# Pairs of tiles from tile 6, row tiles turned later in a step, pair sums used a product later, transfers spread over steps

## The chip, the cores and the metric

The kernel runs on one core of one Trainium2 chip. A core has five engines that run their own instruction streams side by side: TensorE (PE, matrix products), VectorE (DVE), ScalarE (ACT), GpSimd (POOL) and SyncE (SP, which here only issues transfers). Each runs its instructions in the order in which they were written and waits at an instruction until what it needs is there. The metric is the device time of one execution in microseconds (us). Three executions before the change took 1418.22, 1418.4 and 1423.74 us; their median is 1418.4.

## What is computed

A sequence of 2048 rows of 512 features goes through two layers, each a linear-attention block (A) and a gated block (B), with a layernorm ahead of each and a residual around it:

```python
def _B_ref(x, w_in, w_sp, b_sp, w_out):
    z = _gelu(jnp.einsum("bsd,df->bsf", x, w_in))
    z1 = z[..., :Fh]
    z2 = _layernorm(z[..., Fh:], axis=-1)
    g = jnp.einsum("ts,bsf->btf", w_sp, z2) + b_sp[None, :, None]
    return jnp.einsum("bsf,fd->bsd", z1 * g, w_out)

x = A_x
x = x + _A_ref(_layernorm(x, axis=-1), A_wqkv, A_wo)
x = x + _B_ref(_layernorm(x, axis=-1), B_w_in, B_w_sp, B_b_sp, B_w_out)
x = x + _A_ref(_layernorm(x, axis=-1), A_wqkv, A_wo)
x = x + _B_ref(_layernorm(x, axis=-1), B_w_in, B_w_sp, B_b_sp, B_w_out)
```

Fh is 896. The stage that the change is in computes the end of A (query side, output weights, residual), the layernorm, and both halves of `z`: `z1` and the raw `z2`.

## The kernel before

Every matrix product is done in three passes: both operands are split into a high part (ACT rounds it, L101) and a low part (DVE subtracts, L104), and PE multiplies high by high, high by low and low by high (`mm3`, L115 to L117). The 2048 rows are 16 tiles of 128. Each layer runs `P1` (keys, values), `transition`, `P2`, and `P4` (the spatial product and the output). All order is written out by hand: an engine runs its instructions in program order.

`P2.run` goes through steps s = 1 to 18, a software pipeline in which one step works on several tiles:

- `b_high(s)`, `b_low(s)`: the scaled queries of tile s, which went to DRAM and back to be turned by blocks, are transposed on DVE (L351) and split.
- `a2_den`, `a2_mul` (tile s+2), `a` (tile s+3, on POOL, L657): the queries' denominators and scaling. `a2_mul` stores the turned queries to DRAM through SP.
- `c(s-1)`: 12 matmuls with the folded output weights; `c2`: DVE adds the residual (L713); `c_stats`: layernorm statistics on DVE (L287, L289), then three tiny POOL instructions (L291, L292, L294); `c3`: x is stored (L721), ACT normalises (L300), and the row tile is stored turned to DRAM (L336). `xturn.load(s-1)` loads it back through SP, which can only start when the store has landed.
- `d_high(s-2)`, `d_low(s-2)`: DVE transposes that row tile, ACT and DVE split it. Every four tiles make up one block n of `xT`.
- `e`, `e2`, `e3`, `e4` (`singly`): the second half of `z` for one tile (24 matmuls of 448 columns on two banks), its GELU (L927), its layernorm statistics, and the normalisation (with a subtraction on DVE, L938, for tiles 0 to 7).
- `f`: one "z1 unit": 12 matmuls of 512 columns for one of seven feature groups of one block of four tiles, a GELU on ACT (L959), a store (L962). A block's seven units are queued when its fourth tile has been split; up to two are taken per step. So in steps 9, 13 and 17 only one is left in the queue. In layer two the split weights of a unit are loaded from DRAM by POOL (L185, `Parts`), two units ahead: taking one starts the load of the one after the next.

In layer two, from step 7 on, two tiles are done together with seven products where eight would be needed (a Strassen-Winograd scheme on 2x2 blocks). `odd(s)` begins pair m with P1 and P2, `even(s)` goes on with P6, P5, P7, P4 and P3. Each is six matmuls of 448 columns (L804 to L806). P1, P6, P7 and P4 accumulate one after the other in one PSUM bank X, and ACT copies X out after P1 (L849), P6 (L877), P7 (L891) and P4 (L899); DVE adds the other banks (`add`, L816). P6, P5, P7 and P3 need sums of the pair's two row tiles: `block_sums` (four DVE instructions, L762 to L765) and `block_parts` (their splits; P6 and P5 use the first two parts). They need the row split of the pair's second tile, which `d_high` and `d_low` make in the same odd step. The weight sums T1 to T4 are loaded by POOL (L262, `Sums2.fetch`), two per step in steps 2 to 5.

After step 18 `P4.run` first takes the five z1 units that are left, prepares the first operands of the spatial product and finishes the last pair (`finish`), then PE starts the spatial product, whose first step needs all eight PSUM banks.

Of the kernel before, what the change touches and what calls it, by code (L numbers as in the profile page):

```python
# [19 lines left out]
NT = S // P  # L20
# [4 lines left out]
LN_EPS = 1e-5  # L25
PHI_EPS = 1e-6
DEFER = 6


class Slots:  # L30
# [23 lines left out]
def mixer_kernel(ctx: ExitStack, tc: tile.TileContext, x_in, wqkv, wo_d, win1_d, win2_d, wsp_d, bsp_d, wout_d,  # L54
# [17 lines left out]
    def ztag(i, shape, kind, dtype=F32):  # L72
        t = main.tile(shape, dtype, tag=f"z{i}", bufs=1, name=f"z{i}_{kind}")
        ztile[i] = t
        return t
# [27 lines left out]
    def low(l, src, h):  # L103
        nc.vector.tensor_sub(l, src, h.bitcast(F32))  # L104
# [16 lines left out]
    def flush(n=4):  # L121

        for _ in range(min(n, len(stores))):
            d, part, page = stores.popleft()
            nc.sync.dma_start(d, part.bitcast(F32))
            if page is not None:
                pages.put(page)
# [145 lines left out]
    def w_wo():  # L273
        return Weight(bigs, [P, 4, 512], [wo_d[c * P:(c + 1) * P, :] for c in range(4)])
# [4 lines left out]
    def w_in2():  # L279
        return Weight(bigs, [P, 4, FH], [win2_d[f] for f in range(NF)])  # L280
# [75 lines left out]
    class P1:  # L356
        def __init__(self, L):
# [4 lines left out]
            self.wo, self.win2 = w_wo(), w_in2()  # L362
            self.later = deque(range(NT - DEFER, NT))
            self.turn = Turn(f"xt{L}", range(3) if L == 0 else ())
# [156 lines left out]
        def run(self):  # L521
            side = deque()
            for w in (self.wv, self.wo, self.win2):
                side.extend([w] * len(w.pieces))
            side[0].fetch()
            ND = NT - DEFER
            for s in range(1, NT + 2):
                self.loadx(s + 3)
                self.turn.load(s + 1)
                flush()  # L530
                turned = 2 <= s < NT and s not in self.turn.by_pe
                if turned:
                    self.T_high(s)
                if s == 1:
                    if not self.kb:
                        self.K(0)
                    self.K(1)
                elif 2 < s <= NT:
                    self.K(s - 1)
                self.ln_a(s + 2)  # L540
                if turned:
                    self.T_low(s)
                if s <= NT:
                    self.K_phi(s - 1)
                if s <= ND:
                    self.Q(s - 1)
                if s == NT + 1:
                    self.late()
                if s <= NT:
                    self.xsplit(s - 1)  # L550
                    self.K_split(s - 1)
                if s + 1 < NT and s + 1 in self.turn.by_pe:
                    self.T(s + 1)
                self.ln_b(s + 2)
                if s <= ND:
                    self.Q_phi(s - 1)
                if s >= 2:
                    self.Gmm(s - 2)
                if s == NT + 1:
                    self.late_phi()  # L560
                for _ in range(min(len(side), 1 if s < 6 else 2)):
                    side.popleft().piece()
                for w in list(side)[:1 if s < 5 else 2]:
                    w.fetch()
# [71 lines left out]
    class P2:  # L636
# [105 lines left out]
        def d_low(self, i):  # L742
            b, home, h, l = self.dpart
            low(l, b, h)
            if self.sums2 is not None and i >= 4:
                self.rows.append(b)
            else:
                home.put(b)
            n, k = divmod(i, 4)
            if i in self.xB:  # L750
                pages.put(self.xB.pop(i))
            if k == 3:
                self.fnext = [(n, f) for f in range(NF)]
# [63 lines left out]

        def last_quarter(self, m):

            if m < 2:  # L820
                return
            self.add(2 * m, self.HI, self.Z)
            banks.put(self.Z)
            self.gelu(2 * m, self.HI)

        def two(self, step, m):
            if m >= 2:
                step(2 * m)
                step(2 * m + 1)

        def odd(self, s):
            m = (s - 3) // 2
            i = 2 * m
            if s < NT:
                self.b_high(s)
                self.b_low(s)
            self.a2_den(s + 2)
            self.d_high(s - 2)
            self.d_low(s - 2)
            self.two(self.e4, m - 2)  # L840
            self.last_quarter(m - 1)
            if s <= NT:
                self.c(s - 1)
                self.c2(s - 1)
                self.c_stats(s - 1)
            self.X, y = banks.get([P, HF]), banks.get([P, HF])
            self.product(self.X, m, "P1", start=True)
            z = ztag(i, [P, FH], f"z{self.L}")
            nc.scalar.activation(z[:, self.LO], self.X, AF.Copy)  # L849
            self.product(y, m, "P2", start=True, stop=True)  # L850
            self.a2_mul(s + 2)
            if s <= NT:
                self.c3(s - 1)
            self.a(s + 3)
            self.block_sums(m)
            self.add(i, self.LO, y)
            banks.put(y)
            self.block_parts(m)
            self.gelu(i, self.LO)
            self.xturn.load(s - 1)  # L860
            self.f()
            self.f()

        def even(self, s):
            m = (s - 4) // 2
            i, X = 2 * m, self.X
            if s < NT:
                self.b_high(s)
                self.b_low(s)
            self.a2_den(s + 2)  # L870
            if s <= NT:
                self.c(s - 1)
                self.c2(s - 1)
                self.c_stats(s - 1)
            Z = self.Z = banks.get([P, HF])
            self.product(X, m, "P6")
            nc.scalar.activation(ztile[i][:, self.HI], X, AF.Copy)  # L877
            self.product(Z, m, "P5", start=True)
            self.a2_mul(s + 2)
            if s <= NT:  # L880
                self.c3(s - 1)
            self.a(s + 3)
            if s <= NT + 1:
                self.d_high(s - 2)
                self.d_low(s - 2)
            self.f()
            if m >= 3:
                self.e3(i - 2)
            self.product(X, m, "P7")
            z = ztag(i + 1, [P, FH], f"z{self.L}")  # L890
            nc.scalar.activation(z[:, self.HI], X, AF.Copy)  # L891
            self.add(i + 1, self.HI, Z)
            self.gelu(i + 1, self.HI)
            if m >= 3:
                self.e3(i - 1)
            self.xturn.load(s - 1)
            self.f()
            self.product(X, m, "P4", stop=True)
            nc.scalar.activation(z[:, self.LO], X, AF.Gelu_apprx_tanh)  # L899
            banks.put(X)  # L900
            self.product(Z, m, "P3", stop=True)
            pages.put(*self.S_pages)
# [63 lines left out]
        def run(self, sums):  # L966
            for s in range(1, NT + 3):
                self.loadx(s + 1)
                self.qturn.load(s + 1)
                flush()  # L970
                paired = self.sums2 is not None and s >= 7
                if paired:
                    if s == 7:
                        self.e4(3)
                    (self.odd if s % 2 else self.even)(s)
                else:
                    self.singly(s)
                self.fq.extend(self.fnext)
                self.fnext = []
                if self.L == 0:  # L980
                    self.win1.piece(True)
                    self.win1.fetch()
                    if s > 7:
                        sums.tick()
                else:
                    if 2 <= s < 6:
                        self.sums2.fetch(2)
                    if s == 4:
                        self.win1.fetch()
                if s >= NT + 1:  # L990
                    self.p4.fetch(s - NT - 1)
            if self.L == 0:
                self.e4(NT - 1)
            else:
                self.sums2.free()
            self.win2.free()
# [372 lines left out]
    sums = Sums()  # L1369
# [44 lines left out]
```

## Time and profile before

| | |
|---|---|
| median of three runs | 1418.4 us (1418.22 to 1423.74) |
| the profiled execution | 1425.49 us, span 1423.7 us |
| mean granted TensorE clock | 0.992 |
| PE busy | 1395.9 us, 98% of the span |
| DVE, ACT, POOL busy | 910.5, 598.8, 446.2 us |
| stage of the change, layer two (steps 7 to 18 and the last units) | 888.13 to about 1083 us |

The span runs from the first to the last instruction of the program in the profile. Busy time of PE is a sum of modelled, overlapping matmuls; how fast it works is seen from the distance between two starts and from the granted clock (1.00 is full speed, 0.50 half). In a timeline row the first number is the start, the second the duration, and the bracket gives the idle time before it and what ended it. In a row by stretch the columns are: the stretch, its length, then busy time and number of instructions of PE, PE's weight loads, DVE, ACT and POOL, then the granted clock, the share of time the DMA engines were busy, and GB/s. In the list of waits: who waited for whom, the total, how often, the longest.

### The profile page before, as it was taken

The numbers are of one execution on the slowest core, as the hardware profiler recorded it, in microseconds if no ns is written. First come the engines' busy times: TensorE is split into PE (matmuls) and PEld (weight loads), VectorE is DVE, ScalarE is ACT, GpSimd is POOL, SyncE is SP. The second block draws the span as 40 slices with busy tenths as digits, with TensorE's granted clock in tenths as the row PEclk, the third lists the DMA queues.
The fourth block names the chain that finished last, engine by engine and source line by source line (L and its number), as shares of the span: only waits on it lengthen the run. The fifth ranks groups of instructions, "written<-read, shape, count | busy, mean of one in ns | idle before, by whom it ended". The sixth has DMA issues, their size and how long they took to land. (4 is left out here: it accounts for less than half of the span.)

```text
span 1423.7 us, 17853 instructions
## 1 busy us (share of the span) xinstructions
PE 1395.9 (98%) x6234; PEld 1163.2 (82%) x6234; DVE 910.5 (64%) x1321; ACT 598.8 (42%) x930; POOL 446.2 (31%) x559
## 2 busy tenths in 40 slices
PE   9999999999999999999999999898989999999998
PEld 7888888888888888888888888677877888888887
DVE  6785786752746687566677677677637344776642
ACT  6775543333442234232477544434435322342420
POOL 3343444443145523332033335334410000223310
PEclk9999999999999999999999999999999999999999
DMA  5541467866688954457654218767764333544542
GB/s 174 162 134 53 149 211 232 257 216 200 214 267 286 309 188 135 158 197 253 233 156 156 82 37 237 235 186 218 224 186 141 93 100 119 177 132 139 188 134 96
DMA packets 157002, 251.41 MB, mean 177 GB/s; under 512 B 13808, under 2 KB 56048, under 8 KB 156912
## 3 DMA queue, kind: packets, MB, share of 16 engines
q1 hardware_dynamic: 147696, 231.92, 50.6%
q0 software_dynamic: 9216, 18.35, 4.8%
q8 instruction: 49, 0.80, 0.2%
q14 instruction: 41, 0.34, 0.1%
HBM read 174.98 MB, written 75.24 MB: 176 GB/s over the span
## 5 line engine op out<-in xcount | busy, mean ns | idle before, releaser
L1194 PE MATMUL bank<-qd,pg 128*128 128x512 f32 x800 | 311.5, 389 | 2.5 <-DVE z_z L816 2.1
L1195 PE MATMUL bank<-qd,pg 128*128 128x512 f32 x800 | 311.3, 389 | 0.8 <-DVE qd L1160 0.8
L1196 PE MATMUL bank<-qd,pg 128*128 128x512 f32 x800 | 311.2, 389 | 0.0
L1160 DVE TENSOR_TENSOR qd<-qd,qd 128x1024 fp32r<-128x1024 f32 x112 | 158.2, 1413 | 161.8 <-ACT qd L1153 161.2
L1153 ACT ACTIVATE qd<-qd 128x1024 fp32r<-128x1024 f32 x112 | 118.6, 1059 | 241.3 <-DMA qd<-s 104.2
L117 PE MATMUL bank<-qd,pg 128*128 128x512 f32 x496 | 195.7, 395 | 1.2 <-DMA pg<-win 1.1
L1194 PEld LDWEIGHTS bank<-qd,pg 128*128 128x128 f32 x800 | 150.1, 188 | 34.5 <-DVE z_z L816 2.5
L1195 PEld LDWEIGHTS bank<-qd,pg 128*128 128x128 f32 x800 | 150.2, 188 | 32.2 <-DVE qd L1160 1.1
L1196 PEld LDWEIGHTS bank<-qd,pg 128*128 128x128 f32 x800 | 150.2, 188 | 31.2
L1216 POOL TENSOR_TENSOR bg<-bg,pg 128x512 f32<-128x512 f32 x56 | 80.6, 1443 | 298.1 <-DMA pg<-z 280.9
L115 PE MATMUL bank<-qd,pg 128*128 128x512 f32 x400 | 158.7, 397 | 9.1 <-DMA pg<-win 9.1
L116 PE MATMUL bank<-qd,pg 128*128 128x512 f32 x400 | 158.1, 395 | 0.0
L291 POOL TENSOR_SCALAR rs<-mv 128x1 f32<-128x1 f32 x96 | 37.9, 395 | 375.8 <-DVE mv L289 375.3
L1069 POOL TENSOR_TENSOR pg<-pg,pg 128x512 f32<-128x512 f32 x64 | 92.6, 1447 | 97.4 <-DMA pg<-in_wsp_dram 83.8
L300 ACT ACTIVATE pg<-pg,nb,rs 128x512 f32<-128x512 f32 x63 | 51.1, 810 | 148.0 <-POOL nb L294 141.7
L117 PEld LDWEIGHTS bank<-qd,pg 128*128 128x128 f32 x496 | 94.3, 190 | 22.9 <-DMA pg<-win 2.5
L101 ACT ACTIVATE pg<-pg 128x512 fp32r<-128x512 f32 (+2 forms) x88 | 53.6, 610 | 104.5 <-DVE pg L351 49.0
L115 PEld LDWEIGHTS bank<-qd,pg 128*128 128x128 f32 x400 | 76.6, 191 | 25.5 <-DMA pg<-win 10.3
L351 DVE STREAM_TRANSPOSE pg<-pg 128x512 f32<-128x512 f32 x75 | 80.8, 1077 | 19.1 <-DMA pg<-yt 16.0
L116 PEld LDWEIGHTS bank<-qd,pg 128*128 128x128 f32 x400 | 76.4, 191 | 15.8 <-DVE qd L104 0.3
L117 PE MATMUL bank<-wo,qd 128*128 128x512 f32 x224 | 87.3, 390 | 0.0
L115 PE MATMUL bank<-wo,qd 128*128 128x512 f32 x224 | 87.2, 389 | 0.0
(161 smaller groups left out, 2626.1 us busy)
## 6 DMA issues: line engine op xcount, KB each, us to landing
qd<-s SPq DMA_DIRECT2D x64, 512.0 KB, 3.4
qd<-in_wsp_dram SPq DMA_DIRECT2D x48, 512.0 KB, 4.3
pg<-in_wsp_dram SPq DMA_DIRECT2D x64, 256.0 KB, 5.1
s<-pg SPq DMA_DIRECT2D x64, 256.0 KB, 4.9
pg<-x SPq DMA_DIRECT2D x64, 256.0 KB, 3.5
z<-pg SPq DMA_DIRECT2D x56, 256.0 KB, 3.2
pg<-z SPq DMA_DIRECT2D x56, 256.0 KB, 3.8
pg<-win POOLq DMA_DIRECT2D x56, 256.0 KB, 4.8
```

The costliest lines, as they stand in the source:

```text
L101: nc.scalar.activation(h, src, AF.Copy)
L115: nc.tensor.matmul(out, ah, bh, start=start, stop=False)
L116: nc.tensor.matmul(out, ah, bl, start=False, stop=False)
L117: nc.tensor.matmul(out, al, bh, start=False, stop=stop)
L351: nc.vector.transpose(y.rearrange("p c (t m) -> p m c t", m=4), r.rearrange("p (m c j) -> p m c j", m=4, c=4))
L1069: nc.gpsimd.tensor_tensor(t, a, b, op=OP.add)
L1153: nc.scalar.activation(w[:, 0], r, AF.Copy)
L1160: nc.vector.tensor_sub(w[:, 1], r, w[:, 0].bitcast(F32))
L1194: m(out, h[:, o], w[:, 0, j, :], start=start, stop=False, skip_group_check=True)
L1195: m(out, h[:, o], w[:, 1, j, :], start=False, stop=False, skip_group_check=True)
L1196: m(out, l[:, o], w[:, 0, j, :], start=False, stop=stop, skip_group_check=True)
L1216: nc.gpsimd.tensor_tensor(u, u, z1, op=OP.mult)
```

## The change

Nothing is computed in another way except that tiles 4 and 5 of layer two no longer form a pair. The pairs begin with tile 6 (`PAIRED`, step 9). In the odd steps `d_high`, `d_low`, the sums and the parts move behind `c2`, `c_stats`, `a2_mul`, the addition to z, its GELU and the first z1 unit; `e4` moves to the end. In the even steps the first z1 unit, `c3` and the load of the turned tile come ahead of P6, and `d_high`, `d_low` behind P5. In both `xturn.load` follows `c3`. The weight sums are loaded one per step in steps 2 to 9. From step 15 on up to four z1 units' weights are loaded ahead, with one more call of the load after each step. In layer one the first load of spatial weights for `sums` is issued in step 7.

```diff
+PAIRED = 3
-            if self.sums2 is not None and i >= 4:
+            if self.sums2 is not None and i >= 2 * PAIRED:
...
         def odd(self, s):
             self.a2_den(s + 2)
-            self.d_high(s - 2)
-            self.d_low(s - 2)
-            self.two(self.e4, m - 2)
             self.last_quarter(m - 1)
...
             self.a2_mul(s + 2)
             if s <= NT:
                 self.c3(s - 1)
+                self.xturn.load(s - 1)
             self.a(s + 3)
-            self.block_sums(m)
             self.add(i, self.LO, y)
             banks.put(y)
+            self.gelu(i, self.LO)
+            self.f()
+            self.d_high(s - 2)
+            self.d_low(s - 2)
+            self.block_sums(m)
             self.block_parts(m)
-            self.gelu(i, self.LO)
-            self.xturn.load(s - 1)
             self.f()
-            self.f()
+            self.two(self.e4, m - 2)
...
         def even(self, s):
                 self.c_stats(s - 1)
+            self.a2_mul(s + 2)
+            self.f()
+            if s <= NT:
+                self.c3(s - 1)
+                self.xturn.load(s - 1)
+            self.a(s + 3)
             Z = self.Z = banks.get([P, HF])
             self.product(X, m, "P6")
             nc.scalar.activation(ztile[i][:, self.HI], X, AF.Copy)
             self.product(Z, m, "P5", start=True)
-            self.a2_mul(s + 2)
-            if s <= NT:
-                self.c3(s - 1)
-            self.a(s + 3)
+            if m > PAIRED:
+                self.e3(i - 2)
             if s <= NT + 1:
                 self.d_high(s - 2)
                 self.d_low(s - 2)
-            self.f()
-            if m >= 3:
-                self.e3(i - 2)
             self.product(X, m, "P7")
...
-            if m >= 3:
+            if m > PAIRED:
                 self.e3(i - 1)
-            self.xturn.load(s - 1)
             self.f()
             self.product(X, m, "P4", stop=True)
...
         def run(self, sums):
-                paired = self.sums2 is not None and s >= 7
+                paired = self.sums2 is not None and s >= 2 * PAIRED + 3
...
+                    if s == 7:
+                        sums.fetch()
                     if s > 7:
                         sums.tick()
                 else:
-                    if 2 <= s < 6:
-                        self.sums2.fetch(2)
-                    if s == 4:
+                    if 2 <= s < 10:
+                        self.sums2.fetch(1)
+                    if s == NT - 1:
+                        self.win1.ahead = 4
+                    if s == 4 or s >= NT - 1:
                         self.win1.fetch()
```

More of the change, by code (lines that the diff above doesn't have):

```diff
@@ L818, in last_quarter @@
         def last_quarter(self, m):
-            if m < 2:
+            if m < PAIRED:
                 return
@@ L826, in two @@
         def two(self, step, m):
-            if m >= 2:
+            if m >= PAIRED:
                 step(2 * m)
@@ L970, in run @@
                 flush()
-                paired = self.sums2 is not None and s >= 7
+                paired = self.sums2 is not None and s >= 2 * PAIRED + 3
                 if paired:
-                    if s == 7:
-                        self.e4(3)
+                    if s == 2 * PAIRED + 3:
+                        self.e4(s - 4)
                     (self.odd if s % 2 else self.even)(s)
```

## The prediction

> **What bounds the kernel now.** I read the page first, then TensorE's waits, then busy time and clock by stretch, then timelines around each wait. The page says TensorE (PE) is the engine that is always at work; the list of its waits says where it is not.
>
> ```profile
> PE 1395.9 (98%) x6234; PEld 1163.2 (82%) x6234; DVE 910.5 (64%) x1321; ACT 598.8 (42%) x930; POOL 446.2 (31%) x559
> ...
> PE bank L115 <- DMA pg<-win: 9.1, 3, 5.7
> PE bank L804 <- ACT z_s L101: 4.3, 2, 2.3
> ...
> PE bank L1194 <- DVE z_z L816: 2.1, 1, 2.1
> ```
>
> A busy PE can still be slow, so I count starts. Where nothing waits, 512-column matmuls start 0.227 us apart and 448-column ones 0.203. What a stretch lasts beyond its count times these pitches is lost, waits and half clock together. The stretches below are step 7 and 8 of layer two, then the step pairs 9/10, 11/12, 13/14, 15/16, 17/18, then the last five z1 units and the start of the spatial stage (the count in brackets misses a few records; I take counts from the code).
>
> ```profile
> 888.13:923.07 34.94, 28.19 (x115) 22.93 (x114) 22.20 (x38) 15.24 (x26) 13.57 (x24) 0.90 0.79 240
> 923.07:950.20 27.13, 24.81 (x104) 20.14 (x102) 19.23 (x37) 9.16 (x18) 9.05 (x16) 0.94 0.67 199
> 950.20:977.78 27.58, 25.82 (x116) 21.09 (x115) 21.32 (x40) 12.68 (x22) 12.57 (x23) 1.00 0.78 235
> 977.78:1004.33 26.55, 24.21 (x103) 20.21 (x102) 19.01 (x36) 11.86 (x20) 8.18 (x17) 0.94 0.70 199
> 1004.33:1029.26 24.93, 24.93 (x116) 21.40 (x115) 14.98 (x27) 12.34 (x21) 10.22 (x24) 1.00 0.69 201
> 1029.26:1047.46 18.20, 17.28 (x79) 14.49 (x78) 9.93 (x20) 9.45 (x16) 6.07 (x13) 1.00 0.59 174
> 1047.46:1083.00 35.54, 29.40 (x112) 22.42 (x111) 12.80 (x23) 12.88 (x18) 6.57 (x14) 0.90 0.56 176
> ```
>
> Steps 7/8 hold 72 wide and 42 narrow matmuls (24.9 us), so 10.0 us are lost. The pairs with three z1 units hold 60 and 42 (22.1 us): 5.0 lost in 9/10, 4.4 in 13/14. Those with four hold 72 and 42 (24.9): 2.7 in 11/12, nothing in 15/16. Steps 17/18 (36 and 42, 16.7) lose 1.5. In the last stretch the starts lose 6.4 before 1062 and 4.2 after. Sum 34.2 us: all that is to be had here. The waits behind it, and one clock row:
>
> ```profile
> 900.72 0.80 PE L115 MATMUL bank<-qd,pg 128*128 128x512 f32 x1 [5.72 <-DMA pg<-win]
> 935.81 0.47 PE L804 MATMUL bank<-bg,z_s 128*128 128x448 f32 x1 [1.96 <-ACT z_s L101]
> 990.85 0.47 PE L804 MATMUL bank<-bg,z_s 128*128 128x448 f32 x1 [2.29 <-ACT z_s L101]
> 1053.16 0.80 PE L115 MATMUL bank<-qd,pg 128*128 128x512 f32 x1 [2.80 <-DMA pg<-win]
> 936.78:940.18 3.40, 3.40 (x10) 3.01 (x10) 1.76 (x3) 1.46 (x3) 0.00 (x0) 0.50 0.96 197
> ```
>
> A wait of about 2 us or more is mostly followed by 3.4 or 6.8 us at clock 0.50: each costs 1.7 to 3.3 us on top.
>
> **The change part by part.**
>
> *One pair fewer.* Tiles 4 and 5 go through `e` (48 narrow matmuls) instead of seven products (42): 6 x 0.203 = **+1.2 us** on PE. They drop four sums and two splits on DVE and two on ACT; that work lay beside PE.
>
> *Transfers spread.* The weight-sum loads (0.46 MB each) go one per step over steps 2 to 9, not two over 2 to 5. On POOL they stand behind the statistics and the z1 weight loads, and the last pair (T3), issued at the end of step 9, is needed 12 us later, so nothing waits. What they delay now: row 4's turned store left SP at 878.32, could be loaded back only at 884.47 and arrived about 890.2, when DVE's transpose starts. Two sums and four weight pieces lay ahead. Two sums landed 2.1 us apart there and 1.2 ahead of the load, so one sum fewer each time saves 3.3 us. The chain behind it (row split, tile 3's GELU and statistics, POOL's rs, then the weight load at 896.42, landing 4.3 us later) comes that much earlier, about 897.4. Step 7 now has a 4.9 us `e` where P1 and P2 took 2.4, so PE asks at 895.8, not 894.9. Left: 1.6 us for one half of the weights, 0.4 for the other, and 0.5 for half clock in one case of three: **2.5** (0 if the load comes 2 us earlier; 8.5, as now, if the spread does nothing). This replaces the 10.0.
>
> *Four weight pairs ahead from step 15.* The loads that PE waited for at 1053 were issued by POOL only at 1047.06, behind tile 13's statistics. Their successors leave in steps 15 to 18; the last one is asked for 8 us after its issue. The **6.4 us** go. POOL's four extra issues in step 15 (some 2.2 us) end before step 16's statistics. The 4.2 us behind it stay: `prepare` and `finish` still stand behind the last z1 GELU on ACT, and PE still needs the bank that DVE frees there. In layer one `sums.fetch` moves one step earlier; PE has no wait in that stage, so nothing.
>
> *Turning behind the residual, and parts one product later.* P6 now has another z1 unit (2.72 us) ahead of it, so the waits at 935.81 and 990.85 go. But in the even steps `c3` now stands ahead of P6: on ACT, the normalise (L300) precedes the copy of X (L877). P7 accumulates into X and must wait for that copy, and the unit that stood between P5 and P7 is gone. So P7 waits for the normalise, and that for a chain which the rows of 11/12 give:
>
> ```profile
> 964.72 1.09 DVE L351 STREAM_TRANSPOSE pg<-pg 128x512 f32<-128x512 f32 x1
> 966.59 0.69 DVE L104 TENSOR_TENSOR pg<-pg,pg 128x512 fp32r<-128x512 f32 x1 [0.78 <-ACT pg L101]
> ...
> 969.80 0.18 DVE L289 BATCH_NORM_AGGREGATE mv<-st 128x2 f32<-128x6 f32 x1
> ...
> 971.70 0.81 ACT L300 ACTIVATE pg<-pg,nb,rs 128x512 f32<-128x512 f32 x1 [4.71 <-POOL nb L294]
> ```
>
> From the odd step's first z1 unit ending on PE: its GELU on ACT 0.2 + 0.5 (L959 takes 0.57 and overlaps the next by 0.1); the row split queued behind it 0.67 on ACT and 0.6 on DVE (L101, L104); four sums 1.5 (905.97 to 907.44); two low parts 1.3 (L104 x2, 1.29); then the even step's DVE work from its transpose (964.72) to the normalise (971.70) 7.0; normalise 0.73, copy 0.54. Sum 13.0 us. In that time PE has `c`, one unit, P6 and P5 (7.9 us), and a second unit (10.6) in step 11. P7 therefore waits 5.1 us in step 10, plus 0.5 because tile 5's late normalise holds DVE in step 9; 2.4 in step 12; in step 14 the two `e4` of tiles 6 and 7 add 2.0 and the missing denominators take 1.2 away: 13.8 - 7.9 = 5.9. In step 16 there is no transpose and no denominator: nothing. Together 14.0, and half clock after each, 3 x 2.3 (the mean of 2.6 after 900.72, 1.7 after 935.81 and 990.85, 3.3 after 1053.16): **+20.9** (14.0 to 24.2, and 3 more per us of chain). P6 of step 18 keeps a wait of 1.1. This replaces 13.6. Behind P7 on PE stand a z1 unit, P4 and P3; behind the normalise on ACT the copy, a row split and the next GELUs. They move along with it, and no one beyond this pair is made later than PE itself is.
>
> [...]
>
> On SP the even steps' x and turned stores now stand behind one z1 store; that GELU ends 3 us before the normalise, so they lose nothing; past these 3 us the next odd step's split would come later us for us, once 3 more are used up (the turned tile is back 26 to 32 us after the pair's start, wanted at 35). The turned load blocks SP while its store lands (2.5 to 6 us); next are a z1 store and loads wanted a step later. In step 11 POOL's second weight load reuses the page of that step's turned store and holds POOL to some 13 us after the step's start; the next statistics come at 18.
>
> **Sum**: -10.0 - 13.6 - 6.4 + 1.2 + 2.5 + 20.9 + 1.1 = -4.3 us. The profiled execution took 1425.49 us (span 1423.7, 1.8 around it), 7.1 above the median of 1418.4; the difference goes onto the median: **1414 us**. Half a per cent (7.1 us) is about what can be told from no change.
>
> **The rivals.**
> *The copy is in time.* P7 waits nowhere: 20.9 drop out, 1393. For it: every wait that the list names is covered. Against: DVE's order and the 7.0 us, which came out alike in three steps.
> *The spread doesn't help.* Step 7 keeps its 8.5 us: +6.0, 1420. For it: the load also waits for statistics on POOL (6.70 us idle until 895.02). Against: the last link of that chain is a transfer.
> *The VectorE loop sets the period (slower).* Each us more between step 9's row split and the copy of X is paid three times; 1.5 us more turns the gain into a loss. For it: DVE and ACT pass every split to and fro, 0.7 us idle each, and DMA is 70 to 80% busy. At 2.5 us more per pair step 16 waits 2 us too: +10, 1424, and 1428 with the longer half-clock stretch each time. Against: all loads on the chain are due 5 us or more after issue.
>
> **How the numbers follow.** Chances: my forecast 0.55 (its own range 1407 to 1421), copy in time 0.16, spread useless 0.09, VectorE loop 0.20. With each unknown at its end my forecast lies between 1405 (-30.0 + 16.3) and 1427 (start 8.5, waits 17, half clock 10.2, with 2.7 for the rest). Range 1400 to 1427; most of the 1393 case and the top of the loop case are left out. Below 1411.3: the second case and a third of the first, 0.35; above 1425.5: most of the loop case, 0.19; between: 0.46.
>
> **What would show it.** Right: no wait for win weights at the last five units; no wait at P6 in steps 10 and 14; waits at P7 (L804's successor) on ACT's copy in steps 10, 12 and 14, of 5, 2 and 6 us, with clock 0.50 after. Wrong: P7 without waits, or a wait of 5 us left in step 7.

## The result and the profile after

The changed kernel takes **1425.34 us** (median of ten runs, 1422.71 to 1429.97) beside 1420.58 us for the kernel before (ten runs on the same chip, 1417.04 to 1423.74). The ratio is 1.0037, with a 95% interval from 1.0023 to 1.0051. The change makes the kernel some 5 us slower.

The two profiled executions do not show that in their spans (1423.7 us before, 1424.3 after). The execution of the kernel before holds, at 235.42 us in layer one, a wait of 1.46 us on PE, and the granted clock is 0.83 over the ten microseconds from 235 on; the changed kernel's has no such wait there, and its clock over the same ten microseconds is 1.00. So the comparison is made inside the stage of the change, by lost PE time as in the prediction: what a stretch lasts beyond its number of matmuls times 0.227 us (512 columns) or 0.203 us (448 columns).

The page's first line, and PE's waits, in the changed kernel:

```profile
PE 1392.5 (98%) x6240; PEld 1163.3 (82%) x6240; DVE 909.8 (64%) x1312; ACT 598.4 (42%) x925; POOL 448.2 (31%) x559
```

```profile
PE bank L805 <- ACT z_z L884: 18.4, 4, 7.0
PE bank L116 <- DMA pg<-win: 2.6, 1, 2.6
...
PE bank L1199 <- DVE z_z L817: 2.1, 1, 2.1
PE bank L116 <- ACT qd L102: 2.0, 2, 1.2
```

Shares of busy time are as before. The list of waits is another one: weights from DRAM cost 2.6 us, not 9.1, and the waits of P6 for `z_s` have gone. In their place PE waits four times, 18.4 us in all, for the copy after P6 (L884).

Busy time and clock of the changed kernel by stretch, the step pairs 9/10 to 17/18:

```profile
917.63:950.15 32.52, 24.50 (x103) 20.21 (x102) 20.72 (x36) 10.63 (x19) 9.25 (x15) 0.90 0.77 236
950.15:977.62 27.47, 25.16 (x116) 21.32 (x114) 21.00 (x37) 11.10 (x20) 12.34 (x22) 1.00 0.67 201
977.62:1007.55 29.93, 24.52 (x103) 20.70 (x102) 18.54 (x32) 12.84 (x21) 8.04 (x18) 0.89 0.65 185
1007.55:1037.98 30.43, 26.75 (x117) 22.76 (x116) 13.86 (x26) 12.47 (x20) 13.18 (x28) 0.94 0.66 193
1037.98:1056.76 18.78, 17.35 (x78) 14.22 (x77) 11.60 (x22) 9.65 (x15) 4.73 (x10) 1.00 0.49 159
```

| lost PE time, us | before | forecast for after | after |
|---|---|---|---|
| steps 7/8 | 10.1 | 2.5 | 4.5 |
| 9/10 | 5.0 | 7.9 | 10.4 |
| 11/12 | 2.7 | 4.7 | 2.6 |
| 13/14 | 4.4 | 8.2 | 7.8 |
| 15/16 | 0 | 0 | 5.6 |
| 17/18 | 1.5 | 1.1 | 2.1 |
| last five units | 6.4 | 0 | 0 |
| start of the spatial stage | 4.2 | 4.2 | 4.5 |
| sum | 34.3 | 28.6 | 37.5 |

(Steps 7/8 of the kernel before come out at 10.1 us here, where the prediction had 10.0.) With 1.2 us for the pair that is no longer formed, the changed kernel stands at 37.5 + 1.2 - 34.3 = **+4.4 us**. The medians differ by 4.8, so the stage accounts for the result. The account comes from one execution of each kernel, however: for the runs below the same sum differs from the measured change by up to some 3.5 us (the order alone: +9.4 counted, +12.5 measured; the start alone: -7.4 counted, -4.3 measured). That it comes so close here is in part luck.

The rows of PE behind it, in order of time (start, duration, and in the bracket the idle time and what ended it):

```profile
894.68 0.61 PE L116 MATMUL bank<-qd,pg 128*128 128x512 f32 x1 [2.60 <-DMA pg<-win]
926.46 0.50 PE L116 MATMUL bank<-qd,pg 128*128 128x512 f32 x1 [0.79 <-ACT qd L102]
939.43 0.74 PE L805 MATMUL bank<-bg,z_s 128*128 128x448 f32 x1 [7.01 <-ACT z_z L884]
968.38 0.47 PE L805 MATMUL bank<-bg,z_s 128*128 128x448 f32 x1 [2.31 <-ACT z_z L884]
996.23 0.74 PE L805 MATMUL bank<-bg,z_s 128*128 128x448 f32 x1 [5.42 <-ACT z_z L884]
1027.15 0.47 PE L805 MATMUL bank<-bg,pg 128*128 128x448 f32 x1 [3.68 <-ACT z_z L884]
1041.80 0.50 PE L116 MATMUL bank<-qd,pg 128*128 128x512 f32 x1 [1.20 <-ACT qd L102]
```

The rows with L805 are P7 in steps 10, 12, 14 and 16. The first row is the wait left in step 7. The second and the last are the first z1 unit of a block (in steps 10 and 18), which waits for the split of the block's fourth row.

Where step 16's wait comes from stands in the rows of POOL and of SP's queue:

```profile
1010.99 3.27 POOL L186 DMA_DIRECT2D pg<-win  x6 [0.20 <-issue]
1023.43 1.06 POOL L186 DMA_DIRECT2D pg<-win  x2 [9.16 <-DMA z<-pg]
1024.57 0.23 POOL L292 TENSOR_SCALAR rs<-mv 128x1 f32<-128x1 f32 x1
```

```profile
1011.67 0.37 SPq L337 DMA_DIRECT2D yt<-pg  x1
1015.87 0.32 SPq L98 DMA_DIRECT2D pg<-yt  x1
1016.29 1.49 SPq L963 DMA_DIRECT2D z<-pg  x2
```

In step 15 POOL goes on to a fourth pair of weight loads, which reuse a page (a buffer in SBUF) from which a z1 store has yet to read. That store stands on SP behind the load of the turned row, which waits until 1015.87 for its own store to land (issued at 1011.67, 4.1 us to landing); the z1 store is issued at 1016.29 and POOL comes free only at 1023.43, after 9.16 us. Only some 2 us of these pass before the store is issued; nearly all the rest passes until it lands. The two z1 stores issued here take 6.4 us to land, where the median over the whole profile is 3.2; the six weight loads that POOL issued just before them take 7.6, where that median is 5.0:

```profile
pg<-win POOLq DMA_DIRECT2D x6, 256.0 KB, 7.6
z<-pg SPq DMA_DIRECT2D x2, 256.0 KB, 6.4
```

Whether the early loads slowed the store that they then waited for is not shown: no run tests that by itself.

Row 15's `rs` is behind that on POOL, although its statistics were ready at 1020.06 (`mv`, on DVE). Then come the normalise, the copy after P6 and P7.

The rows of 1023.43 (POOL) and 1015.87 (SP) show both waits on the engine that issues, with what is queued behind standing too: POOL is idle for 9.16 us, and row 15's `rs` starts at 1024.57, 4.5 us after its statistics; SP issues nothing from 1012.04 to 1015.87, and the z1 store goes out behind that.

### The profile page after: what moved, and what is told of

Read it like the earlier page. It is cut to its first block, busy times and chain, and to the rows that moved or that the text cites. A ratio compares the mean times of both kernels' runs of the same rounds, so it can differ in the third digit from the quotient of the medians.

```text
span 1424.3 us, 17861 instructions
## 1 busy us (share of the span) xinstructions
PE 1392.5 (98%) x6240; PEld 1163.3 (82%) x6240; DVE 909.8 (64%) x1312; ACT 598.4 (42%) x925; POOL 448.2 (31%) x559
## 4 chain that ended last, share of the span: by engine, by line
PE 88%; DMA 4%; DVE 3%; ACT 2%; POOL 1%; issue 1%; SPq 0%; POOLq 0%; DVEq 0%; ACTq 0%
PE bank L117 16%; PE bank L118 16%; PE bank L116 16%; PE bank L1200 13%; PE bank L1201 12%; PE bank L1199 12%; DMA yt<-pg 1%; DMA z<-pg 1%; DVE st L288 1%; DMA pg<-win 1%; PE bank L805 1%; POOL rs L293 1%; ACT pg L301 1%; DVE pg L714 1%; PE bank L807 0%
## 5 line engine op out<-in xcount | busy, mean ns | idle before, releaser
L118 PE MATMUL bank<-wo,qd 128*128 128x512 f32 x224 | 87.2, 390 | 0.0
L116 PE MATMUL bank<-wo,qd 128*128 128x512 f32 x224 | 87.1, 389 | 0.0
L117 PE MATMUL bank<-wo,qd 128*128 128x512 f32 x224 | 87.1, 389 | 0.0
```

The costliest lines, as they stand in the source:

```text
L116: nc.tensor.matmul(out, ah, bh, start=start, stop=False)
L117: nc.tensor.matmul(out, ah, bl, start=False, stop=False)
L118: nc.tensor.matmul(out, al, bh, start=False, stop=stop)
```

## The experiments

The theory to begin with (A): the loss is made by the order of the even steps, with `c3`'s normalise ahead of the copy that P7 waits for, and by the loads of step 15; the start and the last five units do gain. The main rival (B): the steps are bound by a loop through DVE, ACT, POOL and the transfers, so that a wait taken away comes back at the next product, whatever the order. In each run A and B are as its expectation states them. All runs are given as ratios to the kernel before on the same chip (medians of 1418.3 to 1420.8 us there).

### The copy ahead of c3

```diff
         def even(self, s):
...
             self.f()
-            if s <= NT:
-                self.c3(s - 1)
-                self.xturn.load(s - 1)
-            self.a(s + 3)
             Z = self.Z = banks.get([P, HF])
             self.product(X, m, "P6")
             nc.scalar.activation(ztile[i][:, self.HI], X, AF.Copy)
             self.product(Z, m, "P5", start=True)
+            if s <= NT:
+                self.c3(s - 1)
+                self.xturn.load(s - 1)
+            self.a(s + 3)
```

> The changed kernel, with c3 of the even steps put back behind P5, so that ScalarE copies X after P6 before it normalises. Theory A (P7 waits for the copy because the copy stands behind the normalise): the waits at P7 in steps 10, 12, 14 and 16 (7.2, 2.5, 5.6 and 3.9 us in the changed kernel's profile, some 7 us of half clock behind them) go; the copy after P7 is now behind the normalise, so P4 may wait 2 to 4 us in steps 10 and 14. Time 8 to 16 us below the changed kernel, 1410 to 1417. Theory B (the chain of VectorE and ScalarE sets the length of a pair whatever the order of the copies): the wait moves to P4 at full size, and the time stays within 2 us of the changed kernel, 1423 to 1427.

Measured: 1410.61 us, ratio **0.9925 (0.9912 to 0.9939)**, so 15 us less than the changed kernel by moving one normalise behind one copy. Lost time in the stage falls from 37.5 to 23.0 us. Of step 10, PE and then ACT:

```profile
933.86 0.47 PE L805 MATMUL bank<-bg,z_s 128*128 128x448 f32 x1 [0.22 <-ACT z_z L880]
941.11 0.67 PE L805 MATMUL bank<-bg,qd 128*128 128x448 f32 x1 [3.01 <-ACT z_z L893]
```

```profile
933.27 0.54 ACT L880 ACTIVATE z_z<-bank 128x448 f32<-128x448 f32 x1
939.29 0.81 ACT L301 ACTIVATE pg<-pg,nb,rs 128x512 f32<-128x512 f32 x1 [5.49 <-POOL nb L295]
940.01 0.61 ACT L102 ACTIVATE qd<-pg 128x512 fp32r<-128x512 f32 x1
940.53 0.52 ACT L893 ACTIVATE z_z<-bank 128x448 f32<-128x448 f32 x1
```

The normalise is no earlier (939.29, in the changed kernel 938.14). But the copy after P6 stands ahead of it and ends at 933.81, and P7 waits 0.22 us instead of 7.01. What is left of the same chain moves to P4, which waits 3.01 us for the copy after P7 (L893), behind the same normalise. A part of B is there, then: the wait came back at the next copy, at about two fifths of its size.

### c3 behind P7's copy

```diff
         def even(self, s):
...
             self.f()
-            if s <= NT:
-                self.c3(s - 1)
-                self.xturn.load(s - 1)
             self.a(s + 3)
...
             nc.scalar.activation(z[:, self.HI], X, AF.Copy)
+            if s <= NT:
+                self.c3(s - 1)
+                self.xturn.load(s - 1)
             self.add(i + 1, self.HI, Z)
```

> The changed kernel, with c3 and the load of the turned tile in even steps moved behind P7 and its copy, so that no copy of X stands behind a normalise. Theory A (the order on ScalarE makes the waits of steps 10 to 16): no wait at P7 or P4 for a copy; a pair then lasts what VectorE needs, about 26 us in 9/10 to 13/14 and 25 in 15/16 (32.5, 27.5, 29.9 and 30.4 in the changed kernel): 14 to 18 us below the changed kernel, 1407 to 1412. Theory B (the later normalise makes the turned tile late for the next odd step): waits of 2 us and more at P6 or at a block's first z1 unit take back most of it, 1418 to 1425.

Measured: 1412.84 us, ratio 0.9943 (0.9928 to 0.9958), a little above A's 1407 to 1412. The waits at P4 shrink from 3.5 to 2.9 us, but the row of the even step comes later: the first z1 unit of step 18 waits 4.5 us for row 15's split, where the changed kernel has 1.2. What `c3` hands on has a due time too.

### The order of the steps alone

The new `odd` and `even` with pairs from tile 4, the old loads and nothing else:

```diff
-PAIRED = 3
+PAIRED = 2
...
-                    if s == 7:
-                        sums.fetch()
...
-                    if 2 <= s < 10:
-                        self.sums2.fetch(1)
-                    if s == NT - 1:
-                        self.win1.ahead = 4
-                    if s == 4 or s >= NT - 1:
+                    if 2 <= s < 6:
+                        self.sums2.fetch(2)
+                    if s == 4:
```

> The new order of the odd and even steps alone: pairs from tile 4, weight sums two per step in steps 2 to 5, no further loads ahead, layer one as before. Theory A (the order is what loses: c3's normalise ahead of the copy of X that P7 waits for): P7 waits in steps 8, 10, 12 and 14 on ACT's copy, 2 to 7 us each, with half clock behind most; 4 to 7 us slower, ratio 1.003 to 1.005. Theory B (the order gains by itself, and what loses is its meeting with the other parts): ratio below 0.999.

Measured: 1431.64 us, ratio **1.0091 (1.0074 to 1.0108)**: 12.5 us slower, a loss larger than expected. Its waits at P7:

```profile
PE bank L805 <- ACT z_z L884: 17.7, 4, 5.4
```

In steps 8, 10, 12 and 14 P7 starts 2.7, 5.2, 4.9 and 5.6 us late, and lost time in the stage is 43.7 us. So the order loses by itself, with the old loads too. Step 12 starts P7 4.9 us late here, not 2.5 as in the changed kernel; why was not traced.

### The start alone

The kernel before with `PAIRED = 3` and one weight sum per step:

```diff
+PAIRED = 3
...
-                    if 2 <= s < 6:
-                        self.sums2.fetch(2)
+                    if 2 <= s < 10:
+                        self.sums2.fetch(1)
```

(and `PAIRED` where the pairs' bounds were 2 and 3, as in the change).

> The kernel before, with pairs from tile 6 and the weight sums loaded one per step in steps 2 to 9, and nothing else (old order of the steps, no further loads ahead). Theory A (the start of the stage and the order of the pairs are separate matters): step 7 loses 4 to 5 us instead of 10, one pair fewer costs 1.2, the waits of the later steps stay as before: 4 to 5 us faster, ratio 0.996 to 0.998. Theory B (the start's gain only moves into step 9, where P6 of the first pair now waits for a later row): 1.000 to 1.002.

Measured: 1414.81 us (12 runs), ratio **0.9970 (0.9960 to 0.9980)**, 4.3 us faster. Up to step 9's first product 3.3 us are lost instead of 10.1. P6 of step 10 still waits, 2.6 us (before 1.96). The gain comes without the other parts, as A has it.

### The loads ahead alone, from step 15 and from step 16

```diff
-                    if s == 4:
+                    if s == NT - 1:
+                        self.win1.ahead = 4
+                    if s == 4 or s >= NT - 1:
                         self.win1.fetch()
```

> The kernel before, with nothing but the four weight pairs ahead from step 15 and the extra loads after steps 15 to 18. Theory A (the wait of 2.8 us at 1053 and the 3.3 us of half clock behind it come from the late loads alone, and the page that holds GpSimd in step 15 costs little where P6's copy is ahead of the normalise): 4 to 6.4 us below the kernel before, ratio 0.9955 to 0.997. Theory B (the page holds GpSimd in any order): step 16 gets a new wait of 3 us or more and the ratio is 0.998 to 1.001.

Measured: 1418.84 us, ratio 0.9990 (0.9979 to 1.0001): hardly a gain, as B says, but the new wait is not in step 16, where B had it. The wait at the last five units is gone, and P6 of step 18 waits (the first row is POOL, the second PE):

```profile
1015.24 2.12 POOL L185 DMA_DIRECT2D pg<-win  x4 [2.99 <-DMA yt<-pg]
```

```profile
1034.30 0.47 PE L804 MATMUL bank<-bg,pg 128*128 128x448 f32 x1 [2.69 <-ACT pg L101]
```

POOL holds 2.99 us for a page and issues four more loads before the statistics at 1017.44. In this order the hold is a third of what the changed kernel shows, and what comes late is P6 of step 18, not P7 of step 16. The next kernel begins the same loads one step later (`NT` in place of `NT - 1`, twice).

> The kernel before, with four z1 weight pairs ahead and an extra call of the load after each step from step 16 on, and nothing else of the change. The same part from step 15 on gave 0.999 where 6.4 us had been counted for it. Theory A (the prefetch of step 15 took a page whose z1 store had not left, held POOL, and so made row 15's normalise late, which is what gave the gain back): without the prefetch in step 15 the hold is gone, P6 of step 18 waits 1 us or less instead of 2.85, the wait at the last units stays away, and the full 6.4 us come out: 1413 to 1415 beside 1420, ratio 0.995 to 0.997. Theory B (what the last units gain comes back elsewhere whatever POOL does): ratio 0.998 to 1.001.

Measured: 1413.41 us, ratio **0.9961 (0.9947 to 0.9976)**, 5.7 us faster. POOL has no hold in steps 15 and 16, and the first matmul of P6 in step 18 comes 0.9 us late instead of 2.9. From step 15's first product to the start of the spatial stage 1.4 us are lost, in the run before 4.9. So theory A holds for this part: the extra loads bring about the 6.4 us counted for them, and those of step 15 give most of it back.

In the changed kernel the same edit:

> The changed kernel, with four weight pairs ahead from step 16 on in place of step 15. Theory A (step 16's P7 waits because GpSimd, at the end of step 15, stands 9.2 us before a weight load into a page whose z1 store has not landed, and step 16's rs and nb stand behind it): that wait of 3.9 us and its half clock go, about 5.5 us, time about 1420; the wait at the last five units (6.4 us before the change) stays away, because the loads still leave in steps 16 to 18. Theory B (step 16 waits for the VectorE chain like the other steps): P7 of step 16 keeps 2 us or more, and the time stays at 1423 to 1427.

Measured: 1421.25 us, ratio 1.0010 (0.9999 to 1.0020), 0.0027 below the changed kernel's: some 4 us, where A had 5.5. P7 of step 16 no longer waits; three waits at P7 are left:

```profile
PE bank L805 <- ACT z_z L884: 15.4, 3, 7.6
```

Steps 15 to 18 lose 2.1 us, not 7.7. That the prefetch of step 15 makes step 16's wait is thus shown; that the way goes through the page and SP's order is read from the rows above.

### The waits that are left

Two more causes were tested by moving what is late. In the odd step `d_high` and `d_low` go ahead of `c3` (for the block's first unit), and in layer two's single steps `e3` goes behind the two z1 units, so that on POOL the weight load does not stand behind tile 3's statistics:

```diff
         def odd(self, s):
             self.a2_mul(s + 2)
+            self.d_high(s - 2)
+            self.d_low(s - 2)
             if s <= NT:
                 self.c3(s - 1)
...
             self.f()
-            self.d_high(s - 2)
-            self.d_low(s - 2)
...
         def singly(self, s):
                 self.e2(s - 3)
-                self.e3(s - 3)
+                if self.L == 0:
+                    self.e3(s - 3)
             self.f()
             self.f()
+            if s >= 3 and self.L > 0:
+                self.e3(s - 3)
```

With the copy ahead of c3 and the loads from step 16 these are four moves:

> The changed kernel with the copy of X ahead of c3 in the even steps (as in the run that gave 0.9925), four weight pairs ahead from step 16 instead of 15, d_high and d_low of the odd step right behind a2_mul and ahead of c3 (for the first z1 unit of a block, which waits for the fourth row's split), and in layer two's single steps e3 behind the two z1 units (for the weight load in step 7, which stands on POOL behind tile 3's statistics). Theory A (the four waits are independent, each with its own cause): lost time in the stage goes from 23.1 to 14 to 16 us, 1400 to 1404 beside 1420, ratio 0.986 to 0.989. Theory B (the steps are bound by a loop through DVE, ACT and POOL, and a wait taken away comes back at the next product): 1408 to 1411, ratio 0.992 to 0.994.

Measured: 1405.14 us, ratio 0.9904 (0.9888 to 0.9920), a little above A. Steps 7/8 lose nothing (6.3 us with the copy ahead alone), and no first unit waits for the split. But steps 11/12, which lost nothing with the copy ahead alone, lose 4.5 us, 2.4 of it at P4.

Two of the four (the copy and `e3`):

> Two of the four moves: the copy of X ahead of c3 in the even steps, and in layer two's single steps e3 behind the two z1 units. Theory A (step 7's wait for win weights is set by tile 3's statistics, which stand ahead of the weight load on POOL): PE's wait of 3.83 us near 895 and its half clock go, 6 us in all, and nothing else changes: 1404 to 1406 beside 1420, ratio 0.987 to 0.990. Theory B (what the start gains is lost again in the first two pairs, which then wait for the same transfers): 1408 to 1411.

Measured: 1407.75 us, ratio 0.9913 (0.9898 to 0.9928), between the two expectations and next to B's lower end. The wait near 895 is gone: its cause was tile 3's statistics, ahead of the load on POOL. Of the size I can say less. The profiled executions have 5.4 us less lost time (17.6 against 23.0), the ratios differ by 0.0012, some 2 us, and their intervals overlap.

Three of the four (without the early split):

> The four-move kernel without the earlier row split in the odd steps (so the copy of X first, e3 late, four weight pairs ahead from step 16). Theory A (the early split made step 9's and 11's normalise late, and with it the waits at P4 that the four-move kernel shows in 11/12): steps 11/12 lose 1 us or less instead of 4.5, the first unit of a block waits 1 to 2 us again in steps 10 and 18: 1402 to 1404, ratio 0.986 to 0.988. Theory B (11/12 lose the same 4.5 us because the steps now begin earlier than the transfers): 1406 to 1409, ratio 0.990 to 0.992.

Measured: 1405.57 us, ratio 0.9898 (0.9882 to 0.9913). As a time this lies between the two expectations, but the step that it was made for speaks plainly: 11/12 lose 0.0 us. It is the early split that makes P4 of step 12 wait. In its place the first units of steps 10 and 18 start 0.9 and 1.4 us late again.

The four moves, with `c3` behind P7's copy:

> The four-move kernel with c3 of the even steps behind the copy after P7 instead of behind the copy after P6. Theory A (what is left there is P4 waiting for the copy after P7, behind c3's normalise): the waits of 0.99, 2.21 and 0.7 us at P4 go, 4 to 5 us with the half clock: 1400 to 1402, ratio 0.985 to 0.987. Theory B (the row of the even step then comes back later, and the next odd step's split and the pair sums with it): the loss moves to P6 or to the first z1 unit, 1404 to 1408, ratio 0.989 to 0.992.

Measured: 1403.98 us, ratio 0.9879 (0.9860 to 0.9897). Between A and B: 9/10 lose 2.7 us instead of 4.3, 13/14 0.7 instead of 1.8, but 11/12 lose 5.4. The early row split hides the later row in step 18 (4.5 us with `c3` at this place and no early split).

Then the early split only where a block's fourth row needs it:

```diff
             self.a2_mul(s + 2)
-            self.d_high(s - 2)
-            self.d_low(s - 2)
+            if s % 4 == 1:
+                self.d_high(s - 2)
+                self.d_low(s - 2)
...
             self.f()
+            if s % 4 == 3:
+                self.d_high(s - 2)
+                self.d_low(s - 2)
             self.block_sums(m)
```

> The kernel with c3 behind P7's copy, but with the early row split only in the odd steps whose row is the fourth of a block (9, 13, 17); in 11 and 15 the split stays behind the first z1 unit. Theory A (only a block's first unit needs the early split, and in step 11 it made row 10's normalise and step 12 late): 11/12 lose 1 us or less instead of 5.4, the rest as there: 1399 to 1401, ratio 0.984 to 0.986. Theory B (what 11/12 lose comes from the earlier start of the pairs): ratio 0.987 to 0.989 as before.

Measured: **1399.17 us, ratio 0.9861 (0.9845 to 0.9878)**, as A says, and faster than both kernels of this case. Its waits on PE and its stretches (steps 9/10, 11/12, 13/14):

```profile
PE bank L1206 <- DVE z_z L817: 2.1, 1, 2.1
PE bank L805 <- ACT z_z L885: 1.7, 3, 0.8
PE bank L806 <- DMA bg<-win_T: 0.6, 1, 0.6
```

```profile
913.03:938.03 25.00, 23.29 (x103) 18.89 (x102) 20.65 (x36) 9.85 (x18) 9.25 (x15) 1.00 0.82 246
938.03:962.92 24.89, 24.89 (x116) 21.41 (x114) 19.82 (x34) 10.96 (x19) 12.38 (x22) 1.00 0.88 248
962.92:986.63 23.71, 22.66 (x104) 19.00 (x103) 19.27 (x36) 12.17 (x21) 8.50 (x18) 1.00 0.76 229
```

The three stretches lose 2.9, 0.0 and 1.6 us at full clock; the whole stage loses 10.4 us, of which 4.5 are the start of the spatial stage, which no edit here is aimed at (4.2 to 6.1 in the other runs). The same stretches had DMA busy for 0.76 to 0.88 of the time, more than the changed kernel's 0.65 to 0.77. Neither the transfers nor the loop through DVE and ACT was what held the changed kernel's pairs: the order in which ACT and POOL met them was.

## Why the prediction was wrong

The forecast was 1414 us and more chance for faster than for slower. It came out 1425, inside the range, but slower. Of the 11 us between, 2.2 are the kernel before, whose median is 1420.58 over ten runs and was 1418.4 over three. The rest is the sum, which failed by 8.7 us (-4.3 forecast, +4.4 found). Step by step:

- **The path: right.** "P7 accumulates into X and must wait for that copy": four rows of PE show it, the order alone loses 12.5 us, and the copy ahead of `c3` wins 15. P6's waits at 935.81 and 990.85 went, as said.
- **Step 16, "In step 16 there is no transpose and no denominator: nothing": wrong, +5.6 us**, the largest miss. The working looked at DVE's part of the chain only. The step of it that failed is "POOL's four extra issues in step 15 (some 2.2 us) end before step 16's statistics". Counted was what the issues take, not what they wait for. The last two needed a page whose store was first queued on SP and then slow to land (6.4 us beside a median of 3.2), and POOL stood for 9.16 us. The prediction saw such a hold in step 11 ("holds POOL to some 13 us after the step's start") and did not ask it of the loads that the change adds. This step does not account for the missed sign by itself: without the loads of step 15 the changed kernel is still at 1.0010.
- **Step 10, 5.1 + 0.5 and 2.3 for half clock: 2.5 us short.** The term that was left out is the first z1 unit of a block. The split moved behind the first unit of the odd step, but the unit in the even step is the first of the new block and needs that split: 0.94 + 0.5 us late here, 1.36 + 0.5 in step 18 (forecast there: 1.1 at P6, found 2.1 in the pair). The rest is in this row of DVE in the changed kernel, where the chain was to lose 0.78 us between ACT and DVE:

```profile
933.03 0.69 DVE L105 TENSOR_TENSOR pg<-pg,pg 128x512 fp32r<-128x512 f32 x1 [2.02 <-DMA z<-pg]
```

  Again a page that a z1 store still held, 1.2 us more than counted.
- **Steps 12 and 14: right.** Waits of 2.31 and 5.42 us for 2.4 and 5.9. Step 12 cost 2.1 us less than the sum had, because no half clock followed (granted clock 1.00 from 968.40 to 971.80).
- **The start: right in kind, 2.0 us short.** The forecast was 1.6 + 0.4 + 0.5; found were 2.77 us of late start and 1.7 of half clock (0.53 over the 3.4 us from 894.70, then 0.96), which the sum had taken "in one case of three". As a part alone the start brings 4.3 us.
- **"The 6.4 us go": right.** PE has no wait at the last five units in any kernel with the loads, and from step 16 they bring 5.7 us.
- **The spatial start, 4.2 (found 4.5): as said. One pair fewer, +1.2:** this is counted here as in the prediction, and no run has it alone.

Of the rivals, "the VectorE loop sets the period" gave 1424 and was nearest in time, and it named a wait of 2 us in step 16. It was not the cause: with the loads of step 15 put off, step 16 waits nowhere, while DVE's work is unchanged. "The copy is in time" is refuted by the four waits, and "the spread doesn't help" by 0.9970 for the start alone, with one reserve: fewer pairs and fewer sums per step were not run apart.

The prediction's sum, taken by parts, has +8.4 us for the order (20.9 + 1.1 - 13.6), -6.3 for the start (2.5 - 10.0 + 1.2) and -6.4 for the loads. Measured alone are +12.5, -4.3 and, from the ratio, -1.4 (loads from step 15): +6.8, or +4.1 without the 2.7 us that P7 of step 8 starts late, a step that forms no pair in the changed kernel. Measured together are 4.8. The loads missed most. The intervals of the three parts leave the sum some 3 us either way, so whether the parts act on one another is not shown.

## What to carry to other kernels

When an instruction is moved ahead of another on the same engine, ask what it waits for, not how long it takes: here a normalise of 0.8 us in front of a copy of 0.5 cost some 15 us, because the products accumulate in one bank and wait for the copy. Loads that are issued earlier also need their pages earlier: here a prefetch that reused a page whose store was still queued or under way stopped POOL and everything behind it for 9.16 us (2.99 us in the old order of the steps), and starting it one step later in that order brought 5.7 us instead of 1.4. And for each move list every consumer of what becomes later, those that come once in four steps (here a block's first unit) included.

## What the runs showed of the hardware

A wait of two to four microseconds had no fixed price here. In the changed kernel, the granted clock of the 3.4 us behind the waits of 2.60, 2.31 and 3.68 us was

```profile
894.70:898.10 3.40, 3.40 (x9) 2.46 (x10) 3.03 (x6) 1.74 (x3) 0.44 (x2) 0.53 1.14 382
...
968.40:971.80 3.40, 3.40 (x16) 2.93 (x17) 2.68 (x4) 1.62 (x3) 2.70 (x5) 1.00 0.92 271
...
1027.20:1030.60 3.40, 3.40 (x11) 2.86 (x12) 1.66 (x3) 1.27 (x3) 1.09 (x3) 0.62 0.83 227
```

that is, 0.53, 1.00 and 0.62. At the start of the spatial stage the same wait of 2.10 us stands in the kernels with two and with three moves. Behind it the clock was (two moves, then three):

```profile
1054.90:1058.30 3.40, 3.40 (x9) 2.68 (x10) 3.00 (x8) 2.65 (x4) 1.44 (x3) 0.55 0.20 26
```

```profile
1054.40:1057.80 3.40, 3.40 (x15) 2.82 (x16) 3.00 (x8) 2.65 (x4) 1.44 (x3) 1.00 0.30 106
...
1064.60:1068.00 3.40, 3.40 (x11) 2.66 (x11) 3.37 (x7) 2.00 (x3) 0.00 (x0) 0.61 0.00 0
```

With three moves the slow stretch came ten microseconds later, behind two waits of 0.8 us each. Equal waits, different clocks: in these rows it was not the length of the wait alone that decided, and they don't show what else did. For a sum of this kernel it is safer to give each such wait a half-clock term as a bound, from nothing to the 3.3 us seen in the kernel before (clock 0.50 over the 6.82 us from 1052.83), than the mean of a few.
